# A recomputed written-out order for a fused attention and FFN kernel: other first loads, other eviction engines, other last semaphore

## Chip, core and metric

The kernel runs on one core of a Trainium2 chip. The metric is the device time of one execution in microseconds (us), lower is better. A profiled execution also has a span: the time from its first to its last recorded instruction.

## The reference, cut to what matters

For 8 batches of 8 heads, 576 queries attend to 16 beacon keys and, causally, to 576 keys of width 64. The result is laid out as 4608 rows of 512 and goes through a product of two linear layers and two more linear layers:

```python
k_all = np.concatenate([beacon_k, k], axis=2); v_all = ...      # (8, 8, 592, 64)
scores = scale * np.matmul(q, k_all.transpose(0, 1, 3, 2))      # causal mask after the 16 beacons
a = softmax(scores);  attn = np.matmul(a, v_all)
x = attn.transpose(0, 2, 1, 3).reshape(4608, 512)
h = ((x @ w1) * (x @ w2)) @ w3                                  # 1024 wide
out = h @ w_out                                                 # (4608, 512)
```

## The kernel before

The kernel multiplies `w3` by `w_out` first (Wt = w3·w_out), so that the FFN is `((x@w1)*(x@w2)) @ Wt`. All matmuls are in fp16 with fp32 sums. No loop runs over the work: a string `ORDER` of some two thousand small steps is read from left to right, and each step issues its instructions on a fixed engine. Every engine and every DMA queue takes its own instructions in the order in which the string names them; semaphores join the engines. So the order of the string is the whole schedule. The letters at the end of a step name an engine (`A` ScalarE, `D` VectorE, `P` GpSimd, `S` SyncE), the last number of a matmul step is the PSUM bank (0 to 7; a pair of banks for scores).

The steps, with their lines in the profile:

- Loads. `lq b c`, `lk b c`, `lv b c` load piece c of q, k or v of batch b (L332, L340), `lkb` and `lvb` the beacons (L369, L377, L385). For batch 0, q and k are loaded in another shape (L357), and the very first piece of each is loaded by the queues of SyncE and ScalarE, in fp32. `l1 c` and `l2 c` load a block of 256 columns of `w1` and `w2` (L390), `l3 r` a block of `w3` (L399), `lo a` a block of `w_out` (L402). All but the two first loads are on GpSimd's queue. It has eight semaphores, which its DMAs take in turn, so that a ninth waits for the first.
- Batch 0 and the weights. `cast` puts a loaded piece into fp16 order, `tq`/`tk` transpose it on TensorE (L422 for batch 0, L428 for others), `eq`/`ek` evict it (L296). `tn`/`en` do the same for beacons (L458). `t3 r`, `e3 r` transpose a block of `w3` (L484), `f r a` multiplies a part of it by `w_out` block a (L493), `ew r` evicts a row block of Wt.
- Attention. `s b g` computes group g of 13 score groups of a batch into a pair of banks with 64-row operands (L508), `exp` evicts it through ScalarE into a ring of 8 (L518), `m` masks the diagonal on VectorE (L528), `v b t h` multiplies by v and a ones column (L539), `n` normalises on VectorE (L550, L551). For later batches q and k are transposed by DMA on SyncE's queue (`Dq` L471, `Dk` L477), and so is the attention's output (`TX` L574; on TensorE for batches 0 to 2: `x` L565, `ex`).
- FFN. Rows are taken in nine blocks of 512. `a mc kf` and `b mc kf` are the two first products (L580, four matmuls each); `ea` evicts the one, scaled, to SBUF on ScalarE (L300) or VectorE (L302); `eb` multiplies it by the other on VectorE (L595). `o mc mt` multiplies by Wt (L601, eight matmuls), `eo` evicts (L300 or L302), `st` stores 128 rows (L615) by GpSimd's queue or SyncE's. The last `o` of the program is done in two halves of 256 columns.
- `spin n bank` issues n matmuls of zeros whose result nobody reads (L621).

At the end SyncE waits for the semaphores of all DMA queues and engines in nine instructions of two semaphores each, and then for the barrier (L693). The DMAs of the hardware queues (SyncE's and ScalarE's) take eight semaphores in turn as well; the waits name these eight in a fixed order from the second instruction to the ninth.

Of the kernel before, what the change touches and what calls it, by code (L numbers as in the profile page):

```python
# [62 lines left out]
consts 0; lq 0 0 S; lk 0 0 A; l3 2; consts 1; spin 8 7; l3 4; l3 3; lo 0; lkb 0 P; cast 0 0 q A;  # L63
lo 1; l3 0; consts 2; spin 1 7; tq 0 0 6; cast 0 0 k A; l3 1; eq 0 0 D 6; spin 3 7; tk 0 0 7;
ek 0 0 A 7; spin 2 6; t3 2 6; lq 0 1 P; e3 2 D 6; spin 2 7; t3 4 7; lkb 1; e3 4 D 7; spin 2 6;
t3 3 5; lo 2; e3 3 D 5; spin 2 7; f 4 0 6; lk 0 1 P; tn 0 7; f 2 0 5; lk 1 0 P; en 0 A 7; s 0 0 0;
s 0 1 2; lo 3; exp 0 0 0; f 2 1 5; f 4 1 6; f 3 0 7; exp 0 1 2; m 0 0 0; lv 0 4; s 0 2 0; f 3 1 7;
exp 0 2 0; m 0 0 1; t3 0 4; lk 0 2 P; t3 1 3; e3 0 D 4; cast 0 1 q A; lk 0 3 P; e3 1 D 3; f 0 0 2;
lq 0 2 P; tq 0 1 4; f 0 1 2; eq 0 1 A 4; l3 6; f 4 2 6; f 2 2 5; cast 0 1 k A; lvb 0; f 1 0 4;
l3 5; tk 1 0 3; f 1 1 4; ek 1 0 A 3; f 1 2 4; tk 0 1 3; lq 0 3 P; f 2 3 5; ek 0 1 A 3; lq 1 1 P;  # L70
f 3 2 7; ew 2 D 5; f 3 3 7; cast 0 2 k A; lkb 2; f 1 3 4; ew 3 D 7; f 4 3 6; lv 0 1; cast 0 3 k A;
tk 0 2 5; ew 1 D 4; f 0 2 2; lv 0 0; ek 0 2 A 5; cast 0 2 q D; tk 0 3 7; ew 4 D 6; tq 0 2 4;
ek 0 3 A 7; f 0 3 2; lk 1 4 P; eq 0 2 D 4; t3 6 6; ew 0 A 2; lv 0 3; s 0 3 0; s 0 4 4; s 0 5 2;
e3 6 D 6; exp 0 3 0; lvb 1; f 6 0 7; t3 5 6; cast 0 3 q D; lv 0 2; exp 0 5 2; m 0 1 0; f 6 1 7;
e3 5 D 6; f 6 2 7; l1 3; exp 0 4 4; s 0 6 0; s 0 7 2; m 0 1 1; l3 7; tq 0 3 6; exp 0 7 2; f 6 3 7;
lq 1 0 P; eq 0 3 D 6; f 5 0 5; l2 1; f 5 1 5; ew 6 D 7; exp 0 6 0; tk 1 4 6; f 5 2 5; l1 1;
ek 1 4 D 6; f 5 3 5; m 0 2 0; tq 1 1 6; l1 0; ew 5 A 5; eq 1 1 D 6; v 0 1 0 7; lq 1 3 P; v 0 0 1 5;
n 0 1 0 7; v 0 0 0 6; n 0 0 1 5; l2 0; s 0 8 2; s 0 9 0; s 0 10 4; n 0 0 0 6; lq 1 4 P; exp 0 8 2;
v 0 2 0 7; lk 1 3 P; t3 7 6; n 0 2 0 7; exp 0 10 4; v 0 1 1 3; lk 1 1 P; e3 7 D 6; tq 1 0 7;
exp 0 9 0; s 0 11 4; n 0 1 1 3; f 7 0 6; lq 1 2 P; f 7 1 6; m 0 2 1; exp 0 11 4; s 0 12 2;  # L80
eq 1 0 D 7; f 7 2 6; m 0 3 0; exp 0 12 2; v 0 2 1 7; l1 2; m 0 3 1; f 7 3 6; n 0 2 1 7; v 0 3 1 5;
ew 7 A 6; lk 1 2 P; v 0 3 0 4; n 0 3 1 5; tq 1 3 6; l2 3; n 0 3 0 4; x 0 1 7; eq 1 3 A 6; x 0 2 5;
x 0 3 3; ex 0 1 D 7; ex 0 2 A 5; x 0 4 6; x 0 0 4; lv 1 4; ex 0 3 D 3; ex 0 4 A 6; ex 0 0 D 4;
tq 1 4 7; l2 2; eq 1 4 A 7; a 0 3 5; lv 1 0; b 0 0 6; ea 0 3 A 5; lv 1 2; b 0 3 7; lv 1 3; a 0 1 5;
eb 0 3 7; tk 1 1 4; lq 2 0 P; ea 0 1 A 5; tk 1 3 7; ek 1 1 D 4; tq 1 2 3; b 0 1 2; ek 1 3 A 7;
lv 1 1; eq 1 2 D 3; tk 1 2 7; eb 0 1 2; a 0 0 5; ek 1 2 A 7; lk 2 0 P; a 0 2 7; ea 0 0 A 5;
lk 2 2 P; eb 0 0 6; s 1 0 0; s 1 1 2; s 1 2 4; ea 0 2 A 7; lq 2 2 P; exp 1 1 2; b 0 2 6; lq 2 1 P;
a 0 4 7; exp 1 2 4; m 1 0 1; lq 2 4 P; eb 0 2 6; b 0 4 3; exp 1 0 0; lk 2 1 P; ea 0 4 D 7; a 0 6 6;
eb 0 4 3; lk 2 3 P; s 1 3 4; s 1 4 0; s 1 5 2; m 1 0 0; ea 0 6 A 6; lq 2 3 P; exp 1 3 4; tq 2 0 7;
v 1 0 0 6; eq 2 0 D 7; lv 2 0; n 1 0 0 6; tk 2 0 7; exp 1 5 2; a 0 5 5; lk 2 4 P; ek 2 0 D 7;  # L90
m 1 1 0; exp 1 4 0; lk 3 2 P; tk 2 2 6; b 0 5 7; m 1 1 1; ek 2 2 D 6; lk 3 0 P; ea 0 5 A 5;
s 1 6 2; s 1 7 0; s 1 8 4; eb 0 5 7; exp 1 6 2; lv 2 1; Dq 2 4; v 1 1 0 6; tq 2 2 7; n 1 1 0 6;
lq 3 4 P; exp 1 8 4; tq 2 1 3; v 1 0 1 2; lv 2 3; eq 2 2 D 7; tk 2 1 6; eq 2 1 D 3; exp 1 7 0;
tk 2 3 7; lk 3 3 P; b 0 7 5; ek 2 1 D 6; ek 2 3 D 7; lkb 3; v 1 1 1 6; n 1 0 1 2; tq 2 3 7;
a 0 7 4; lv 2 4; n 1 1 1 6; eq 2 3 A 7; m 1 2 1; tk 2 4 7; lv 2 2; b 0 6 6; ea 0 7 A 4; ek 2 4 D 7;
m 1 2 0; lq 3 3 P; s 1 9 0; s 1 10 2; eb 0 7 5; exp 1 9 0; v 1 2 0 7; lvb 2; eb 0 6 6; o 0 1 5;
lk 3 1 P; n 1 2 0 7; exp 1 10 2; lq 4 1 P; m 1 3 0; v 1 2 1 7; eo 0 1 A 5; lq 3 1 P; s 1 11 0;
s 1 12 2; s 2 0 4; n 1 2 1 7; exp 1 11 0; st 0 1 P; Dk 3 2; v 1 3 0 6; lq 4 3 P; o 0 0 7;
n 1 3 0 6; exp 2 0 4; Dk 3 0; m 1 3 1; exp 1 12 2; m 2 0 0; s 2 1 0; s 2 2 4; s 2 3 2; eo 0 0 D 7;
Dq 3 3; exp 2 1 0; st 0 0 P; x 1 0 6; v 2 0 0 7; ex 1 0 D 6; exp 2 2 4; Dq 3 4; s 2 4 0; n 2 0 0 7;  # L100
v 1 3 1 6; m 2 0 1; o 0 2 7; exp 2 4 0; lvb 3; n 1 3 1 6; Dk 3 1; lq 3 2 P; exp 2 3 2; lv 3 0;
Dq 3 1; x 1 3 6; eo 0 2 D 7; x 1 2 5; ex 1 3 A 6; o 0 3 4; lq 3 0 P; ex 1 2 D 5; Dk 3 3; m 2 1 0;
st 0 2 P; lk 3 4 P; v 2 1 0 7; eo 0 3 A 4; x 1 1 6; n 2 1 0 7; lkb 4; x 1 4 5; v 2 0 1 3;
ex 1 1 A 6; lk 4 0 P; ex 1 4 D 5; s 2 5 0; s 2 6 4; n 2 0 1 3; exp 2 5 0; a 1 4 6; lk 4 1 P;
a 1 3 7; lv 3 1; exp 2 6 4; Dq 3 2; m 2 1 1; ea 1 4 D 6; lv 3 3; s 2 7 2; s 2 8 0; s 2 9 4;
ea 1 3 A 7; m 2 2 0; exp 2 7 2; b 1 4 6; v 2 2 0 7; lq 4 2 P; exp 2 9 4; eb 1 4 6; v 2 1 1 3;
Dq 3 0; n 2 2 0 7; a 1 0 2; exp 2 8 0; lv 3 2; n 2 1 1 3; b 1 0 6; ea 1 0 A 2; m 2 2 1; lv 3 4;
s 2 10 4; s 2 11 0; s 2 12 2; eb 1 0 6; Dk 3 4; lq 4 0 P; exp 2 10 4; b 1 1 7; m 2 3 0; lk 4 3 P;
exp 2 11 0; Dq 4 3; v 2 3 0 6; v 2 2 1 5; n 2 3 0 6; exp 2 12 2; a 1 1 4; Dk 4 0; n 2 2 1 5;
lq 5 1 P; x 2 0 6; ea 1 1 A 4; m 2 3 1; x 2 4 3; a 1 2 5; Dq 4 1; ex 2 4 D 3; ex 2 0 A 6; eb 1 1 7;  # L110
v 2 3 1 4; lk 4 2 P; b 1 3 6; Dk 4 1; n 2 3 1 4; b 1 2 7; eb 1 3 6; lkb 5; x 2 1 4; ea 1 2 A 5;
x 2 3 6; ex 2 1 D 4; ex 2 3 A 6; x 2 2 3; a 1 5 5; eb 1 2 7; lk 4 4 P; ex 2 2 A 3; a 1 6 6;
ea 1 5 D 5; Dq 4 2; s 3 0 0; s 3 1 2; s 3 2 4; ea 1 6 A 6; lq 4 4 P; exp 3 1 2; a 2 0 7; lv 4 3;
a 2 3 6; exp 3 2 4; m 3 0 1; ea 2 0 D 7; b 1 5 3; exp 3 0 0; lk 5 1 P; b 1 6 7; eb 1 5 3; Dq 4 0;
m 3 0 0; ea 2 3 A 6; s 3 3 4; s 3 4 0; s 3 5 2; eb 1 6 7; exp 3 3 4; lv 4 4; v 3 0 0 6; Dk 4 3;
a 1 7 7; n 3 0 0 6; exp 3 4 0; m 3 1 0; b 1 7 5; lvb 4; ea 1 7 D 7; exp 3 5 2; v 3 0 1 6; eb 1 7 5;
s 3 6 0; s 3 7 2; s 3 8 4; n 3 0 1 6; lv 4 1; exp 3 6 0; v 3 1 0 7; m 3 1 1; Dk 4 2; o 1 1 6;
lv 4 0; exp 3 8 4; m 3 2 0; n 3 1 0 7; lv 4 2; Dk 4 4; exp 3 7 2; m 3 2 1; v 3 2 0 7; lq 5 0 P;
eo 1 1 D 6; s 3 9 0; s 3 10 4; s 3 11 2; Dq 4 4; n 3 2 0 7; exp 3 9 0; v 3 1 1 6; st 1 1 P;
o 1 0 7; exp 3 10 4; m 3 3 0; n 3 1 1 6; exp 3 11 2; st 0 3 P; v 3 2 1 6; eo 1 0 D 7; v 3 3 0 5;  # L120
m 3 3 1; b 2 0 4; st 1 0 P; n 3 3 0 5; a 2 1 7; eb 2 0 4; TX 3 0; b 2 3 5; n 3 2 1 6; ea 2 1 A 7;
TX 3 4; b 2 1 7; eb 2 3 5; eb 2 1 7; s 3 12 0; s 4 0 2; s 4 1 4; exp 3 12 0; Dq 5 1; a 2 4 6;
exp 4 0 2; v 3 3 1 7; Dk 5 1; ea 2 4 D 6; s 4 2 0; s 4 3 2; lv 5 3; exp 4 1 4; m 4 0 0; a 2 6 6;
n 3 3 1 7; Dq 5 0; lq 6 3 P; exp 4 3 2; m 4 0 1; v 4 0 0 5; a 2 7 7; lk 5 2 P; ea 2 6 D 6; TX 3 3;
exp 4 2 0; m 4 1 0; o 1 2 4; lk 5 4 P; ea 2 7 D 7; lq 5 4 P; TX 3 2; n 4 0 0 5; lq 5 2 P;
v 4 1 0 7; eo 1 2 A 4; TX 3 1; lq 5 3 P; b 2 4 6; n 4 1 0 7; lk 5 0 P; a 2 2 5; eb 2 4 6; lvb 5;
b 2 2 7; ea 2 2 A 5; lk 5 3 P; b 2 6 6; eb 2 2 7; s 4 4 2; s 4 5 0; s 4 6 4; eb 2 6 6; exp 4 4 2;
lq 6 1 P; b 2 7 7; Dk 5 2; exp 4 6 4; lk 6 2 P; v 4 0 1 6; eb 2 7 7; o 1 3 3; Dk 5 4; lv 5 1;
exp 4 5 0; m 4 2 0; n 4 0 1 6; m 4 1 1; Dq 5 4; v 4 2 0 7; eo 1 3 A 3; st 1 2 P; s 4 7 4; s 4 8 0;
s 4 9 2; n 4 2 0 7; exp 4 7 4; Dq 5 2; b 2 5 6; st 1 3 P; exp 4 9 2; v 4 1 1 7; Dq 5 3; a 2 5 5;  # L130
n 4 1 1 7; exp 4 8 0; a 3 3 4; m 4 3 0; ea 2 5 A 5; Dk 5 0; m 4 2 1; b 3 2 7; eb 2 5 6; ea 3 3 A 4;
s 4 10 2; s 4 11 0; s 4 12 4; exp 4 10 2; Dk 5 3; b 3 3 6; exp 4 12 4; b 3 1 3; eb 3 3 6; Dq 6 3;
exp 4 11 0; a 3 0 2; Dq 6 1; v 4 2 1 6; m 4 3 1; ea 3 0 A 2; v 4 3 0 5; n 4 2 1 6; v 4 3 1 4;
Dk 6 2; a 3 5 2; n 4 3 0 5; lv 6 1; n 4 3 1 4; b 3 5 6; TX 4 0; ea 3 5 A 2; lv 5 4; lv 6 0;
# [56 lines left out]
def kernel(  # L191
# [13 lines left out]
    nc = tc.nc  # L205
    B, H, S, D = q.shape
    Nb = beacon_k.shape[2]
    P = 128
# [80 lines left out]
    def bank(n):  # L289
        return shape(n, "one")  # L290
# [407 lines left out]
```

## Time and profile before

| what | us |
|---|---|
| median of 5 runs | 292.9 (292.36 to 295.09) |
| time of the profiled execution | 293.42 |
| its span | 291.7 |
| TensorE busy | 284.6 |
| ScalarE busy / VectorE busy / GpSimd busy | 163.5 / 154.4 / 133.5 |
| first matmul of zeros / first score exponential | 1.26 / 14.02 |
| first FFN matmul (L580) | 43.23 |
| last eviction starts | 288.25 |

The time of the profiled execution is 1.7 us above its span, and 0.5 us above the median. A busy TensorE is not TensorE at its peak, since matmuls are pipelined and their ends are modelled; the distance from start to start is what a matmul costs in a dense stream.

### The profile page before, as it was taken

Reading aid. Unit: us, or ns where it says so; the run is one execution under the profiler, and the core shown is the slowest. Engines: PE = TensorE matmul, PEld = TensorE weight load, DVE = VectorE, ACT = ScalarE, POOL = GpSimd, SP = SyncE. Lnnn points to the kernel's source line nnn. Section 1 sums busy time; section 2 is a strip of 40 time slices with the busy share of each in tenths; the row PEclk is TensorE's granted clock in tenths of the full one; section 3 lists DMA queues with packets and bytes.
Section 4 is the critical chain, followed back from the end, with each engine's and each line's share of the span. In section 5 each row is a group of like instructions: output and inputs, shape, how many; then the busy total and the mean of one; then the engine's idle time right before and its main releaser. Section 6 shows DMA issues by size and latency. Waiting matters only on the chain.

```text
span 291.7 us, 7029 instructions
## 1 busy us (share of the span) xinstructions
PE 284.6 (98%) x2904; PEld 155.4 (53%) x2904; DVE 154.4 (53%) x344; ACT 163.5 (56%) x214; POOL 133.5 (46%) x186
## 2 busy tenths in 40 slices
PE   7999989999999999999999999999999999999995
PEld 2555755566656565565445545555455545444443
DVE  3338774786667577655456634634546653144500
ACT  3178664868685884477265626845475553232232
POOL 8569878997876460960966601940011001000000
PEclk9999999999999999999999999999999999999999
DMA  7999999999999999999999993999324014200033
GB/s 167 198 196 160 170 175 176 155 131 151 199 179 144 138 140 197 132 148 201 142 167 171 165 173 88 119 153 221 47 91 111 0 29 124 74 2 0 0 145 144
DMA packets 154319, 38.84 MB, mean 133 GB/s; under 512 B 144048, under 2 KB 149936, under 8 KB 154288
## 3 DMA queue, kind: packets, MB, share of 16 engines
q0 software_dynamic: 114720, 26.19, 104.1%
q1 hardware_dynamic: 39360, 11.92, 26.8%
q8 instruction: 22, 0.36, 0.5%
q10 hardware_dynamic: 208, 0.29, 0.3%
q14 instruction: 9, 0.07, 0.1%
HBM read 39.32 MB, written 9.44 MB: 167 GB/s over the span
## 4 chain that ended last, share of the span: by engine, by line
PE 84%; DMA 8%; POOL 5%; ACT 1%; issue 1%; DVE 0%; POOLq 0%
PE one L580 43%; PE one L601 21%; PE one L539 9%; PE pair L508 8%; DMA q<-in_q_dram 3%; DMA k<-in_k_dram 3%; DMA wo<-in_moe_w_out_dram 2%; PE one L428 1%; POOL va L340 1%; PE one L565 1%; POOL w L390 1%; POOL xT L399 1%; ACT ring L518 1%; POOL q L332 1%; POOL st L357 0%
## 5 line engine op out<-in xcount | busy, mean ns | idle before, releaser
L580 PE MATMUL one<-xT,w 128*128 128x512 f16 x576 | 133.0, 379 | 0.4 <-DVE xT L296 0.4
L518 ACT ACTIVATE ring<-pair 128x1024 f16<-128x1024 f32 x104 | 99.1, 1026 | 14.7 <-PE pair L508 14.4
L580 PEld LDWEIGHTS <-w 128*128 128x128 f16 x576 | 53.2, 98 | 60.1 <-issue 2.5
L595 DVE TENSOR_TENSOR gT<-one,asb 128x512 f16<-128x512 f32 x72 | 49.4, 690 | 55.1 <-PE one L580 41.1
L601 PE MATMUL one<-Wt,gT 128*128 128x512 f16 (+1 forms) x296 | 66.3, 373 | 0.0
L300 ACT ACTIVATE asb<-one 128x512 f32<-128x512 f32 x55 | 32.9, 598 | 58.9 <-PE one L580 37.3
L615 POOL DMA_DIRECT2D out_dram<-st x26 | 14.7, 566 | 68.2 <-DVE st L302 25.6
L601 PEld LDWEIGHTS <-gT 128*128 128x128 f16 x296 | 27.8, 98 | 30.3 <-issue 0.5
L340 POOL DMA_DIRECT2D va<-in_v_dram x40 | 34.1, 856 | 20.7 <-PE one L539 14.3
L539 PEld LDWEIGHTS <-ring 128*128 128x128 f16 x960 | 34.8, 98 | 9.8 <-issue 1.7
L539 PE MATMUL one<-va,ring 128*128 128x65 f16 x960 | 37.7, 193 | 0.1
L300 ACT ACTIVATE st<-one 128x512 f32<-128x512 f32 (+1 forms) x26 | 15.1, 581 | 34.4 <-PE one L601 34.4
L551 DVE TENSOR_TENSOR x<-one,rd 128x384 f16<-128x384 f32 (+1 forms) x64 | 31.4, 491 | 2.2
L340 POOL DMA_DIRECT2D k<-in_k_dram x35 | 29.9, 859 | 5.1 <-DMA k<-in_k_dram 1.5
L332 POOL DMA_DIRECT2D q<-in_q_dram x35 | 30.1, 864 | 2.9 <-DMA va<-in_v_dram 1.3
L508 PE MATMUL pair<-qT,kT 64*128 64x80 f16 (+4 forms) x736 | 30.1, 225 | 0.1
L508 PEld LDWEIGHTS <-kT 64*128 64x128 f16 x736 | 19.9, 95 | 13.9 <-issue 10.2
L528 DVE TENSOR_TENSOR ring<-ring,MD 128x768 f16<-128x768 f16 x32 | 17.7, 553 | 10.2 <-ACT ring L518 10.2
L550 DVE RECIPROCAL rd<-one 128x6 f32<-128x6 f32 (+1 forms) x64 | 11.8, 185 | 20.4 <-PE one L539 20.2
L528 DVE TENSOR_TENSOR ring<-ring,MX 128x384 f16<-128x384 f16 x32 | 11.3, 353 | 10.5 <-ACT ring L518 10.4
L493 PE MATMUL one<-wo,gT 128*128 128x512 f16 x56 | 14.9, 380 | 0.4 <-DVE gT L296 0.3
L302 DVE TENSOR_SCALAR asb<-one 128x512 f32<-128x512 f32 x17 | 11.7, 688 | 3.5 <-PE one L580 3.5
(60 smaller groups left out, 130.7 us busy)
## 6 DMA issues: line engine op xcount, KB each, us to landing
out_dram<-st POOLq DMA_DIRECT2D x26, 256.0 KB, 6.4
q<-in_q_dram POOLq DMA_DIRECT2D x28, 128.0 KB, 6.9
va<-in_v_dram POOLq DMA_DIRECT2D x24, 128.0 KB, 7.0
k<-in_k_dram POOLq DMA_DIRECT2D x21, 128.0 KB, 7.2
out_dram<-st SPq DMA_DIRECT2D x9, 256.0 KB, 2.0
xT<-in_moe_w_dram POOLq DMA_DIRECT2D x8, 256.0 KB, 6.2
w<-in_moe_w_dram POOLq DMA_DIRECT2D x8, 256.0 KB, 7.2
wo<-in_moe_w_out_dram POOLq DMA_DIRECT2D x4, 256.0 KB, 7.5
```

What stands on the lines that cost most here:

```text
L300: nc.scalar.activation(dst, src, AF.Copy, scale=by)
L332: nc.gpsimd.dma_start(dst[:rows, c], src[b, :, ds(c * P, rows), :].rearrange("h s d -> s h d"))
L340: nc.gpsimd.dma_start(dst[ds(p0, rows), c], src[b, :, ds(s0, rows), :].rearrange("h s d -> s h d"))
L493: nc.tensor.matmul(bank(n), wT(r)[:, a, rt % 2, :], wo16[:, rt, :], start=(rt == 0), stop=(rt == NFT - 1),)
L508: nc.tensor.matmul(shape(n, "pair")[:, hh, ds(col, w)], kT[ds(hh * 64, 64), t, ts(jt, P)], qT[ds(hh * 64, 64), t, ds(q0, w)],)
L518: nc.scalar.activation(held(b, g)[:, :, 0:GW], shape(n, "pair"), AF.Exp, scale=scale)
L528: nc.vector.tensor_tensor(blk, blk, msk, ALU.mult)
L539: nc.tensor.matmul(pv[:, 2 * at + hh, 0 : D + 1], held(b, g)[:, hh, ds(col, P)], va[:, jt, 2 * t + hh, 0 : D + 1], start=(jt == 0), stop=( ...
L551: nc.vector.tensor_tensor(x16s[b % NB2][:, ds(2 * h, ni), ts(t, P)].rearrange("p i (h d) -> p i h d", h=2), pv[:, 0 : 2 * ni, 0:D].rearran ...
L580: nc.tensor.matmul(bank(n), w12[:, kt, ds(i * DF + kf * P, P)], xT[:, kt, ds(mc * 512, 512)], start=(kt == 0), stop=(kt == NKT - 1),)
L595: nc.vector.tensor_tensor(gTs[mc % 2][:, kf, :], bank(n), asb[slot["asb", (mc, kf)]], ALU.mult)
L601: nc.tensor.matmul(bank(n)[:, 0:w], gTs[mc % 2][:, kf, ts(mt, P)], Wt[:, kf, ds(c0, w)], start=(kf == 0), stop=(kf == NFT - 1),)
```

## The change

The string `ORDER` is replaced by another one with the same work in it. The first load of k now goes to SyncE's queue and that of q to ScalarE's, the other way round from before. The order of the loads on GpSimd's queue, of the matmul groups, of the evictions and stores is new nearly everywhere, and so are many bank numbers. Counted over the string: matmuls of zeros 20 → 18 (and `spin` can now write into bank 0); `tk` transposes on TensorE 14 → 12, `Dk` by DMA 25 → 27; `ea` on ScalarE 55 → 36 and on VectorE 17 → 36; `eo` on ScalarE 26 → 21 and on VectorE 11 → 16; `cast` on VectorE 2 → 5; `e3` on ScalarE 0 → 3; `ew` on ScalarE 3 → 7; stores by GpSimd's queue 26 → 29 and by SyncE's 11 → 8. Runs of adjacent `s` groups, as TensorE sees them: 39 → 41. The eight semaphores of the hardware queues are taken in turn by the two first loads, the DMA transposes and SyncE's stores: 2 + 76 + 11 = 89 before, 2 + 78 + 8 = 88 now. So the last store took the first semaphore, which the second of the nine final waits names, and now takes the eighth, which the ninth names.

```diff
 ORDER = """
-consts 0; lq 0 0 S; lk 0 0 A; l3 2; consts 1; spin 8 7; l3 4; l3 3; lo 0; lkb 0 P; cast 0 0 q A;
-lo 1; l3 0; consts 2; spin 1 7; tq 0 0 6; cast 0 0 k A; l3 1; eq 0 0 D 6; spin 3 7; tk 0 0 7;
-ek 0 0 A 7; spin 2 6; t3 2 6; lq 0 1 P; e3 2 D 6; spin 2 7; t3 4 7; lkb 1; e3 4 D 7; spin 2 6;
-t3 3 5; lo 2; e3 3 D 5; spin 2 7; f 4 0 6; lk 0 1 P; tn 0 7; f 2 0 5; lk 1 0 P; en 0 A 7; s 0 0 0;
...
+consts 0; lk 0 0 S; lq 0 0 A; l3 3; consts 1; spin 8 7; lkb 1; lkb 0 P; l3 4; lk 0 1 P; lq 0 1 P;
+cast 0 0 k A; lo 0; consts 2; cast 0 0 q D; spin 2 7; tk 0 0 6; lo 1; tq 0 0 7; ek 0 0 A 6;
+eq 0 0 D 7; spin 1 0; t3 3 5; lvb 0; tn 0 6; lo 2; e3 3 A 5; l3 6; spin 3 7; t3 4 4; en 0 A 6;
+l3 0; s 0 0 0; s 0 1 2; e3 4 A 4; cast 0 1 k D; lk 0 3 P; tk 0 1 6; cast 0 1 q D; l3 2; exp 0 0 0;
...
+ex 0 3 D 6; ex 0 2 A 3; lv 1 2; s 1 0 0; s 1 1 4; s 1 2 2; ex 0 1 D 7; exp 1 0 0; a 0 4 6; l1 3;
+exp 1 1 4; m 1 0 0; l2 2; a 0 0 7; ea 0 4 D 6; l2 3; exp 1 2 2; tq 2 0 5; m 1 0 1; a 0 5 6;
...
+b 0 4 4; n 1 1 0 5; b 0 2 3; eb 0 4 4; lq 2 3 P; b 0 5 5; ea 0 2 A 6; ea 0 3 D 7; lk 2 3 P;
...
-o 7 0 7 0 256; eo 8 1 A 6; st 8 1 S; eo 7 0 A 7 0 256; st 7 0 S 0 256; o 7 0 5 256 256;
-eo 7 0 A 5 256 256; st 7 0 S 256 256
+eo 8 1 A 6; st 8 1 S; eo 8 0 A 7 0 256; st 8 0 S 0 256; o 8 0 5 256 256; eo 8 0 A 5 256 256;
+st 8 0 S 256 256
 """
...
     def spin(reps, n):
         for _ in range(reps):
-            nc.tensor.matmul(bank(n), zeros[:, 0:P], zeros)
+            nc.tensor.matmul(bank(n) if n else tiles[0][:, 0, :], zeros[:, 0:P], zeros)
```

## The prediction

> **What bounds the kernel now.** I read the page first, then the chain of waits in order of time, the groups of instructions, and last SyncE's waits.
>
> ```profile
> span 291.7 us, 7029 instructions
> PE 284.6 (98%) x2904; PEld 155.4 (53%) x2904; DVE 154.4 (53%) x344; ACT 163.5 (56%) x214; POOL 133.5 (46%) x186
> ...
> DMA  7999999999999999999999993999324014200033
> ...
> q0 software_dynamic: 114720, 26.19, 104.1%
> ```
>
> TensorE is busy nearly throughout, the eviction engines little over half. The DMA row is at 9 for the first 24 slices: GpSimd's load queue (q0) is full.
>
> ```profile
> 3.43 7.21 DMA wo<-in_moe_w_out_dram
> ...
> 11.58 8.09 DMA k<-in_k_dram
> ...
> 32.15 8.89 DMA q<-in_q_dram
> 41.08 0.40 PE one L428 x4
> ...
> 95.22 0.77 PE pair L508 x22
> 95.99 3.56 PE one L580 x16
> ...
> 110.47 3.46 PE one L580 x16
> ...
> 274.38 13.85 PE one L601 x72
> 288.25 0.38 ACT st L300
> ```
>
> The chain has two parts. Up to 41 us it runs over load landings: start plus duration says when a load is there, 10.64, 19.67 and 41.04 us. Counted along the string, 1024, 2480 and 6192 KB of GpSimd's stream have then landed: 161 and then 174 KB per us. This is my clock for loads. After 43 us it is TensorE alone to 288.2. One more thing is seen in it: the same 16 matmuls take 3.56 behind a run of score groups and 3.46 elsewhere. Leaving a run costs 0.10, and the third group of a run is as much longer than the others in the records: about 0.19 for each run.
>
> **TensorE's sum.** Start-to-start distances in a dense stretch: `a` and `b` 0.863 each (144), `o` 1.726 (35, and two halves of 0.873), `v` 0.367 and 0.548 (32 of each), `s` 0.22 to 0.24 (104), `f` 0.43 (32), `t3` 0.447 (8), small transposes 0.14 to 0.26, `spin` 0.216 (20). The sum is 270.1. To it come the start at 1.26; 39 score runs at 0.19, 7.4; and 4.9 for matmuls before 10.1 us, where the trace's clock record grants half speed (nine matmuls of zeros take 0.43 each). That is 283.6. The last matmul slot really ends at 288.05, so TensorE stands still for 4.4 in all. About 3.1 of it lies before 47 us (0.9 before the first transposes at 5.95, 0.5 for an eviction at 17, 0.7 and 0.5 around the landing at 41.04), 1.3 after.
>
> After: 18 matmuls of zeros and two `tk` of 0.22 fewer, 269.2; 41 runs, 7.8; cold part 4.6; start 1.26. That is 282.9, **0.7 less**. What then decides is how long TensorE stands still in the new order.
>
> **Loads.** I put the new load order on the landing record of the old (same cumulated KB, same time) and compare with the place of the first use in TensorE's unhindered sum. Up to 18 us every load is early by 0.3 to 2. Then it turns: `tk 1 2` at 29.9 needs KB 4672, there at 31.9; `tk 1 4` at 37.9 needs KB 6160, at 40.6; `b 0 0` at 46.8 comes 1.9 before its block; `b 0 4` at 49.8 needs the third `w2` block, KB 8240, which lands at 52.6 (the chain's own rate gives 41.04 + 2048/174 = 52.8). From there on the loads gain: `tk 2 2` 2.4, `tk 2 4` 2.4. These waits don't add up, the latest rules: TensorE stands still **2.8** up to `b 0 4`. What else is slow before it has this cover: the chain of six exponentials (1.03 each, from about 11.9 behind an `e3` on ScalarE) that makes banks free about 1 late at 18 us; no `e3` on ScalarE is in the trace, so I take its plain copies, 0.59 for 512 and 0.64 for 576 columns, which give about 1.0 for 1024, and at the least VectorE's 0.69. The cast of the first q on VectorE lies between VectorE's 0.35 (fp16 source) and ScalarE's 0.83 (fp32): either is over before q's transposes can start behind k's at 6.4. If the cover went, the exponentials would cost 1.0. The new `spin 2 0` writes bank 0 and so waits for the exponential of `s 0 3` (about 17.0, due 16.4), and `t3 0` and all of TensorE's queue behind it: 0.6 under the same cover.
>
> **Evictions.** The change moves 19 `ea` and 5 `eo` to VectorE.
>
> ```profile
> L518 ACT ACTIVATE ring<-pair 128x1024 f16<-128x1024 f32 x104 | 99.1, 1026 | 14.7 <-PE pair L508 14.4
> L300 ACT ACTIVATE asb<-one 128x512 f32<-128x512 f32 x55 | 32.9, 598 | 58.9 <-PE one L580 37.3
> L302 DVE TENSOR_SCALAR asb<-one 128x512 f32<-128x512 f32 x17 | 11.7, 688 | 3.5 <-PE one L580 3.5
> ```
>
> ScalarE is relieved of 24 × 0.6 = 14, VectorE takes 24 × 0.69 = 16.6 and gives some `ew`: about 150 and 169 of 292. In no stretch of 10 us after 40 us does either get over 9.5. So sums cost nothing; what costs are places where a bank is used again too soon. I compared each distance with eviction plus 0.25: after 55 us the new order is short at `s 3 4` (0.5), `s 1 9` (0.4), three `ea` on VectorE (0.1 each) and two `v` (0.2): 1.4 by sum. The same list for the old order gives 0.8 and the trace 1.3, of which 0.7 is dust of under 0.1. I take 1.0 + 0.7 = **1.7**; bounds 0.7 and 3.
>
> DMA transposes: SyncE's queue issues one each 1.3 and they land after 2.4 to 9. The tightest new uses are `s 3 0` (about 1.6 to spare), `s 7 0` and `a 5 1` (about 1, both within the error). I take 0, up to 2. Three more stores on GpSimd's queue and three fewer on SyncE's: 0.57 of issue each, at places where that queue has nothing due within 10 us; 0.
>
> **The end.** The last `o`, its eviction and its store keep their form.
>
> ```profile
> SPq L693 <- DMA out_dram<-st: 1.3, 1, 1.3
> SPq L693 <- PEq L693: 0.7, 2, 0.5
> ```
>
> The 1.3 is the landing of the last store. It is waited for by the second of nine instructions (released at 290.36 in the records), and the seven behind it come at 0.061 each. In the new order these seven are passed while the store is under way: **0.43 less**, the surest term. 3.65 from the last matmul slot to the end becomes 3.2.
>
> **Sum.** 282.9 + 2.8 + 1.7 + 3.2 = 290.6 against a span of 291.7: 1.1 less. The profiled execution took 293.42 and the median of the runs is 292.9; I carry the difference to the median: **291.8**.
>
> **Two rules of the skill.** (1) In the trace VectorE's copy of a batch-0 piece ran at 24.16 to 24.74 beside two v loads issued on GpSimd in 0.86 each, just the mean of that row (856 ns). The Trainium skill, "SBUF — State Buffer", section "SBUF: two separate sides", says that GpSimd can't write its descriptors while a VectorE copy holds the port pair that they share. That speaks against this change, which puts three more `cast` on VectorE where the load stream rules. By the rule 3 × 0.58 = 1.7 of the stream could be lost, and the gain of 1.1 would turn into a loss of 0.6; by the row nothing. I take the row, since up to eight loads are under way, and keep 1.7 for the range. (2) The clock: the record grants full speed at 10.1. "TensorE: Matmul & The Clock Gate", Part 1, says that the clock follows activity in a free-running window of about 3.4 us. The new order stands still for 0.4 instead of 0.9 before the first transposes. A grant one window earlier would save 1.7 of the cold part, one later would cost as much. The trace can't tell; either way `b 0 4` waits for 52.6, so I take 0.
>
> **Rivals.**
>
> *The stream's stalls vanish* (chance 0.2). A part of the old landing record is one-off: the load of k at 11.58 took 8.09 and landed 1.9 after its forerunner, where its size is worth 0.7. If that comes from what lay beside it and does not recur, all later landings are 1.2 earlier: 2.8 becomes 1.6, and with it the time 290.6. Against it: the stream has the same loads and the same full queue.
>
> *The stream comes late* (0.25, slower). The new order leans on the stream at over a dozen places and has 368 KB more ahead of the last needed `w2` block than the old (8240 against 7872 KB). From `tk 1 4` to `b 0 4` any further delay is passed on one to one. One more step like the 1.2 above, and the 1.7 of the port rule, makes 2.9: 291.8 + 2.9 = 294.7. It is slower by over 0.5% once the block lands after 52.6 + 1.1 + 1.5 = 55.2. For it: the queue's share of 104%. Against it: the rate held within 161 to 174 over 30 us.
>
> *The change doesn't do what it says* at the end: if another semaphore were the last to come, 0.43 is lost, 292.2. The built order has the last store on the last hardware semaphore, so 0.05, within the main case.
>
> **Chances.** About 0.5% (1.5 us) is what a measurement of this kernel can tell from no change. Main case 0.55: 291.8, own range 290.4 to 293.3, of which 0.2 is faster by over 0.5%, 0.33 within, 0.02 slower. First rival 0.2, all faster. Second 0.25: 0.22 slower, 0.03 within. Sum: faster 0.40, same 0.36, slower 0.24. The range that leaves out 2 in 10 goes from 289.4 (first rival, late stalls at their bound of 0.7, 0.2 for the spread of a median) to 295.0 (the second, 0.3 for that spread).
>
> **Right or wrong.** Right: the last `w2` block lands at 52 to 53.5 and L580 idles before it; about 41 short excesses at score runs; no TensorE wait over 0.6 after 60; SyncE's last data wait directly ahead of the barrier. Wrong: TensorE idle over 4 before 55 us (the stream), or waits of over 1 us on `TX` or DMA-transposed q and k (SyncE's queue), or on VectorE's `asb` (evictions).

## The result, and the profile after

| | before | after |
|---|---|---|
| median, us | 293.36 (74 runs) | 292.2 (39 runs) |
| lowest to highest | 291.59 to 296.98 | 291.1 to 295.71 |
| ratio of after to before | | 0.9964, 95% interval 0.9951 to 0.9977 |
| profiled execution / its span | 293.42 / 291.7 | 291.4 / 289.7 |
| last matmul slot ends / from there to the end of the span | 288.05 / 3.65 | 286.46 / 3.22 |

The changed kernel is faster by 0.36%, about 1.05 us. The ratio is that of the fast runs, which leaves out the one run of the 39 in the slower state; the quotient of the two medians is 0.9960. Forecast were 1.1 us and 291.8. The median of before over 74 runs is 0.46 above that of the first five, which is where the absolute figure missed by 0.4.

The page of the kernel after, parts 1 to 3, the lines that answer to those shown of before:

```profile
span 289.7 us, 6996 instructions
PE 283.3 (98%) x2894; PEld 153.7 (53%) x2894; DVE 169.4 (58%) x366; ACT 148.5 (51%) x190; POOL 135.3 (47%) x189
...
DMA  8999999999999999999999981799950111043003
...
q0 software_dynamic: 114960, 26.98, 101.8%
```

TensorE is as full as before with 1.3 us less of busy time. ScalarE and VectorE have changed places (163.5 and 154.4 before). The load queue fills the same first 24 slices. (`ORDER` has 1189 steps before and 1187 after, fewer than the two thousand that were given above.)

The chain of waits of the kernel after, in order of time (start, us, what), two windows:

```profile
9.35 8.28 DMA st<-in_k_dram
17.66 0.37 DVE o16k L296
...
43.34 1.83 PE one L580 x8
...
50.65 0.86 PE one L580 x4
51.51 0.36 PE one L539 x12
51.87 3.52 PE one L580 x16
```

```profile
279.91 6.72 PE one L601 x39
286.64 0.02 issue
286.66 0.38 ACT st L300
```

The chain before ran over load landings up to the one at 41.04. Here the last one is a piece of k at 17.63, and from there the chain runs over TensorE and its evictions. That doesn't mean that loads have stopped mattering: the third `w2` block lands at 51.73 in the trace's DMA records, and `b 0 4`, the group at 51.77, starts 0.05 later. In the timeline of TensorE:

```profile
51.35 0.53 PE L539 MATMUL one<-va,ring 128*128 128x65 f16 x12
51.77 2.55 PE L580 MATMUL one<-xT,w 128*128 128x512 f16 x11
```

From the `v` to `b 0 4` it is 0.43, where 0.37 is the undisturbed distance. So the wait for the block is only 0.06 here: TensorE has stood still at earlier places (for 0.2 us at 30.97, for a piece of k, among others) and comes just as the block lands.

Groups of instructions of the kernel after:

```profile
L518 ACT ACTIVATE ring<-pair 128x1024 f16<-128x1024 f32 x104 | 99.1, 1026 | 29.5 <-PE pair L508 28.8
...
L300 ACT ACTIVATE asb<-one 128x512 f32<-128x512 f32 x36 | 21.4, 603 | 58.1 <-DVE gT L595 27.1
...
L302 DVE TENSOR_SCALAR asb<-one 128x512 f32<-128x512 f32 x36 | 24.7, 690 | 20.9 <-PE one L580 20.5
```

The durations are those of before (1026, 603 and 690 ns); 19 evictions have moved. ScalarE now sits idle for 28.8 us waiting for scores, before for 14.4: relief that nobody needed.

What TensorE itself waited for, and SyncE's waits at the end (`SPq` is SyncE's sequencer), both of the kernel after (engine, line, releaser: us in total, times, longest):

```profile
PE one L565 <- ACT ring L518: 0.4, 1, 0.4
...
PE one L484 <- DMA xT<-in_moe_w_dram: 0.3, 1, 0.3
```

```profile
SPq L693 <- DMA out_dram<-st: 0.8, 1, 0.8
SPq L693 <- PEq L693: 0.7, 2, 0.5
```

After the first 20 us, no wait of TensorE is over 0.6. The wait for the last store was 1.3 and is 0.8, because the other waits of that place are passed in the meantime.

### The profile page after: what moved, and what is told of

Read it like the earlier page. It is cut to its first block, busy times and chain, and to the rows that moved or that the text cites. A ratio compares the mean times of both kernels' runs of the same rounds, so it can differ in the third digit from the quotient of the medians.

```text
span 289.7 us, 6996 instructions
## 1 busy us (share of the span) xinstructions
PE 283.3 (98%) x2894; PEld 153.7 (53%) x2894; DVE 169.4 (58%) x366; ACT 148.5 (51%) x190; POOL 135.3 (47%) x189
## 4 chain that ended last, share of the span: by engine, by line
PE 91%; DMA 3%; POOL 3%; ACT 1%; DVE 1%; issue 0%; POOLq 0%; DVEq 0%; ACTq 0%
PE one L580 44%; PE one L601 22%; PE one L539 10%; PE pair L508 9%; PE one L493 3%; DMA st<-in_k_dram 3%; PE one L428 1%; PE one L565 1%; POOL xT L399 1%; ACT ring L518 1%; PE one L484 1%; POOL wo L402 1%; PE one L422 0%; POOL st L357 0%; DVE qT L296 0%
## 5 line engine op out<-in xcount | busy, mean ns | idle before, releaser
L580 PE MATMUL one<-xT,w 128*128 128x512 f16 x576 | 134.4, 379 | 0.0
L518 ACT ACTIVATE ring<-pair 128x1024 f16<-128x1024 f32 x104 | 99.1, 1026 | 29.5 <-PE pair L508 28.8
L615 POOL DMA_DIRECT2D out_dram<-st x29 | 16.6, 572 | 93.9 <-ACT st L300 50.9
L300 ACT ACTIVATE asb<-one 128x512 f32<-128x512 f32 x36 | 21.4, 603 | 58.1 <-DVE gT L595 27.1
L302 DVE TENSOR_SCALAR asb<-one 128x512 f32<-128x512 f32 x36 | 24.7, 690 | 20.9 <-PE one L580 20.5
L551 DVE TENSOR_TENSOR x<-one,rd 128x256 f16<-128x256 f32 (+1 forms) x64 | 31.4, 491 | 2.2
L300 ACT ACTIVATE st<-one 128x512 f32<-128x512 f32 (+1 forms) x21 | 12.2, 581 | 35.3 <-PE one L601 35.3
L550 DVE RECIPROCAL rd<-one 128x4 f32<-128x4 f32 (+1 forms) x64 | 11.8, 184 | 13.5 <-PE one L539 11.1
L302 DVE TENSOR_SCALAR st<-one 128x512 f32<-128x512 f32 x16 | 11.1, 691 | 14.3 <-PE one L601 14.3
```

What stands on the lines that cost most here:

```text
L300: nc.scalar.activation(dst, src, AF.Copy, scale=by)
L302: nc.vector.tensor_scalar(dst, src, by, None, ALU.mult)
L518: nc.scalar.activation(held(b, g)[:, :, 0:GW], shape(n, "pair"), AF.Exp, scale=scale)
L551: nc.vector.tensor_tensor(x16s[b % NB2][:, ds(2 * h, ni), ts(t, P)].rearrange("p i (h d) -> p i h d", h=2), pv[:, 0 : 2 * ni, 0:D].rearran ...
L580: nc.tensor.matmul(bank(n), w12[:, kt, ds(i * DF + kf * P, P)], xT[:, kt, ds(mc * 512, 512)], start=(kt == 0), stop=(kt == NKT - 1),)
```

## Experiments

Every ratio is to the kernel before, timed on the same chip; the changed kernel's own 0.9964 is the other reference, from runs of its own, so two ratios with overlapping intervals are not told apart. Line numbers in three kernels are one less, since their string is a line shorter.

**The last semaphore, done alone and undone.** One store near the end on the other queue turns the count of hardware DMAs from 89 to 88 in the old order, or from 88 to 89 in the new.

```diff
 # b_tail: kernel before
-eo 6 2 A 6; st 6 2 S;
+eo 6 2 A 6; st 6 2 P;
 # a_notail: kernel after
-TX 7 1; st 6 2 P; eb 7 6 6;
+TX 7 1; st 6 2 S; eb 7 6 6;
```

> The order before with one store (`st 6 2`) moved from SyncE's queue to GpSimd's, so that the hardware queues carry 88 DMAs and the last store takes the semaphore that is waited for last. Theory (a fixed end term): 0.43 us less than before (0.15%), SyncE's waits behind the landing shrink from eight to one. Rival (the end is set by the landing and the barrier alone): no change.

> The changed order with one store (`st 6 2`) moved to SyncE's queue: 89 DMAs on the hardware queues, so the last store's semaphore is again the second one waited for. Theory: 0.43 us more than the changed kernel, about 0.6 us under before. Rival (the gain lies wholly in the order): as the changed kernel, 1.05 under before.

Measured: 0.9984 (0.9965 to 1.0003) and 0.9982 (0.9958 to 1.0006). The one gives 0.16% to the old order, the other takes 0.18% from the new; expected were 0.15% both times. Each interval alone still reaches no change. The trace is sharper. From the landing of the last store to the end of the span: 1.36 us before, 1.36 in the undone kernel, 0.92 after, 0.92 in the one done alone. That is 0.44, forecast 0.43. SyncE's last waits in the undone kernel:

```profile
SPq L693 <- DMA out_dram<-st: 1.3, 1, 1.3
```

What is left of the change without its semaphore is about 0.5 us, again with no change inside its interval.

**The evictions put back.** In FFN blocks 5 to 8, 16 `ea` and 9 `eo` go back from VectorE to ScalarE.

```diff
-Dk 7 3; a 5 7 6; m 6 3 0; ea 5 3 D 2;
+Dk 7 3; a 5 7 6; m 6 3 0; ea 5 3 A 2;
 ...
-exp 7 2 2; a 6 0 6; m 7 1 0; eo 5 2 D 7;
+exp 7 2 2; a 6 0 6; m 7 1 0; eo 5 2 A 7;
```

> The changed order with the 16 `ea` and 9 `eo` that it gives to VectorE in row blocks 5 to 8 put back on ScalarE (52 and 30 on ScalarE, near the 55 and 26 of before). Theory (evictions lie beside TensorE's work in this stretch): within 0.3 us of the changed kernel. Rival (the choice of engines is where the gain comes from): the gain of 1.05 us goes, 293.4. Other rival (VectorE's 0.69 against 0.60 costs at every close reuse of a bank): 0.3 to 1 us faster than the changed kernel.

Measured: 0.9966 (0.9945 to 0.9986), nearly the changed kernel's own value. The rival that the gain lies in the choice of engines is excluded, since the interval stays below 1; an effect of 0.3 us either way is not, since the interval reaches 0.6 us to both sides. But this kernel's one profiled execution has a span of 292.0, 2.3 more than that of the changed kernel (it is the slowest of its 22 runs, and the changed kernel's is the fourth fastest of 39). TensorE's waits in it say why:

```profile
PE one L484 <- DMA xT<-in_moe_w_dram: 1.3, 1, 1.3
...
PE pair L508 <- DMA kT<-k: 1.1, 1, 1.1
PE one L580 <- DMA xT<-x: 0.5, 1, 0.5
```

The first is a load in the first 20 us. Neither of the last two is an eviction. Both are DMA transposes that landed late, at places which the edit doesn't touch in the order of the queue. They led to the last experiment below.

**More load.** A second copy of the third `w2` block (256 KB) is loaded ahead of `l1 0`.

```diff
-exp 0 9 2; m 0 2 1; l1 0; s 0 11 0;
+exp 0 9 2; m 0 2 1; l2 2; l1 0; s 0 11 0;
```

> The changed order with the third block of w2 loaded twice, the additional 256 KB ahead of the first block of w1 in GpSimd's stream. Theory (from `tk 1 4` to `b 0 4` TensorE follows the stream): all later loads land 1.4 us later and so does everything behind them: 1.2 to 1.5 us more than the changed kernel. Rival (other waits decide and the loads have slack): under 0.4 us more.

Measured: 1.0014 (0.9985 to 1.0043), 0.5% or 1.46 us over the changed kernel. In the timeline of TensorE (start, us, engine, line, operation; in brackets the idle time before it and what ended it) the wait stands at the place that was forecast:

```profile
52.12 0.53 PE L539 MATMUL one<-va,ring 128*128 128x65 f16 x12
53.00 1.47 PE L580 MATMUL one<-xT,w 128*128 128x512 f16 x6 [0.35 <-DMA w<-in_moe_w_dram]
```

The block lands at 52.96 instead of 51.73, and `b 0 4` starts right behind it. So more load ahead of this block passes on to the time. The size fits what 256 KB are worth at the 174 KB per us of the old order (1.47 us), but the interval is some 0.9 us to either side.

**The first two queues.** Swapped back in the new order, and swapped alone in the old.

```diff
 # a_swap: kernel after
-consts 0; lk 0 0 S; lq 0 0 A;
+consts 0; lk 0 0 A; lq 0 0 S;
 # b_swap: kernel before
-consts 0; lq 0 0 S; lk 0 0 A;
+consts 0; lq 0 0 A; lk 0 0 S;
```

> The changed kernel with the first two loads on each other's queue again, k on ScalarE's and q on SyncE's. Theory (what the first 10 us gain or lose is swallowed at the load waits up to `b 0 4`): ratio 0.9964 within 0.001. Rival (the queue of the first k sets the start, and the start passes to the end): 0.3 us or more slower, ratio 0.9975 or above.

> The kernel before with its first two loads on each other's queue (q on ScalarE's, k on SyncE's), its order as it was. Theory (the start is swallowed at the load waits): ratio 1.0000 within 0.0015. Rival (the first queues themselves are the gain of the change, or the loss where the order is made for the other landing): 0.3 us or more, ratio below 0.999 or above 1.001.

Measured: 0.9971 (0.9943 to 0.9999) and 1.0002 (0.9976 to 1.0029). Both are within the theory, but the first interval is too wide to exclude a loss of 0.3 us. Its `b 0 4` starts at 52.26, inside what kernels with the new order show without the swap (51.69 to 52.48). The old order shows no gain from the other landing by itself.

**Less load ahead of the block, and a wait of 0.57 taken away.** The second edit was aimed at the longest late wait of the changed kernel, 0.57 over TensorE's own cost, of which the timeline shows 0.41 as idle:

```profile
99.24 0.62 PE L565 MATMUL one<-ident,x 128*128 128x128 f16 x8
100.26 0.38 PE L565 MATMUL one<-ident,x 128*128 128x128 f16 x4 [0.41 <-ACT ring L518]
```

```diff
 # a_relief
-lq 2 0 P; v 0 3 0 7; ... l2 3; exp 1 2 2; tq 2 0 5; ... eq 2 0 D 5;
-tk 2 2 6; b 0 3 7; ek 2 2 A 6; ... s 1 8 4; eb 0 3 7; exp 1 6 0; tq 2 1 6;
+v 0 3 0 7; ... l2 3; lq 2 0 P; exp 1 2 2; ...
+b 0 3 7; tk 2 2 6; ek 2 2 A 6; ... s 1 8 4; tq 2 0 6; eq 2 0 D 6; eb 0 3 7; exp 1 6 0; tq 2 1 6;
 # a_fix
-x 2 3 6; x 2 1 7; ... ex 2 1 D 7; exp 3 5 4; x 2 2 3; v 3 0 1 7; ... n 3 0 1 7; ... ex 2 3 A 6;
+x 2 3 6; ex 2 3 D 6; x 2 1 7; ... ex 2 1 D 7; v 3 0 1 6; exp 3 5 4; x 2 2 3; ... n 3 0 1 6; ...
 # a_best: both
```

> The changed kernel with one more load of q (part 0 of block 2, 256 KB) moved from ahead of the third w2 block to behind the fourth, and the transposes that need it, and those of k of part 2, moved behind `b 0 3`. Theory (the load stream sets when `b 0 4` runs): the third block lands about 0.8 us sooner than 52.4, and what is gained is what that leaves until the next load that TensorE waits for, 0.1 to 0.4 us: ratio 0.9950 to 0.9960. Rival (the stream isn't the bound there, the order behind it is): ratio 0.9964 as for the changed kernel, `b 0 4` starting no sooner. Also possible: the moved load is now late for its own transposes, ratio 0.997 or more, and a wait is then seen at `tq 2 0`.

> The changed kernel with the wait of 0.57 us near 99.5 us taken away: `x 2 2` into banks 3 comes behind `v 3 0 1`, so that `exp 3 4` has read its banks by then, and `ex 2 3` goes to VectorE right behind its matmul. Theory (a wait in mid kernel, with no load behind it, passes to the end at full size): the wait of 0.57 is gone, 0.5 us less, ratio about 0.9947. Rival (it turns up later, at `tq`, `s 7 0` or another consumer of transposed blocks, which come at their own time): ratio 0.9964, with as much standing still later.

> Both edits together: the later load of q with its transposes, and the other order near 99.5 us. Theory: the two gains add, 0.6 to 0.9 us less than the changed kernel, ratio 0.9933 to 0.9943. Rival (the waits for transposed q and k near 130 and 210 us, 0.2 to 1.3 us in the runs so far, take it back, since TensorE comes there sooner): ratio 0.9950 to 0.9964.

Measured: 0.9994 (0.9965 to 1.0023), 0.9956 (0.9931 to 0.9980), 0.9997 (0.9973 to 1.0021). The first expectation has the load as 256 KB; it is 128. The load edit failed, and neither by a late block nor by late transposes. `b 0 4` starts at 51.99 with its block there since 51.24. The loss comes 8 us later, in the first kernel's timeline of TensorE:

```profile
58.49 0.40 PE L428 MATMUL one<-ident,q 128*128 128x128 f16 x4
59.47 0.38 PE L428 MATMUL one<-ident,q 128*128 128x128 f16 x4 [0.58 <-DVE qT L296]
60.06 1.67 PE L580 MATMUL one<-xT,w 128*128 128x512 f16 x7 [0.21 <-DVE gT L595]
```

I had put two transposes one behind the other into bank 6. The second waits for VectorE to read the first, and the eviction behind it is late too: 1.1 us over TensorE's own cost at the two. The other edit took 0.11 of its 0.57: now `v 3 0 1` waits for `ex 2 3` (0.29 idle). Its 0.9956 is 0.0008 below the changed kernel, which the interval doesn't tell from nothing.

**The transposes' queue.** In the profiles so far, TensorE lost 0 to 1.27 us at `s 7 0` and 0 to 0.74 at `a 3 0`. Two transposes that have time are moved behind those that `a 3 0` needs, and one behind the last k piece that `s 7 0` needs:

```diff
 # a_sp: kernel after
-... Dq 7 3; exp 6 3 4; ... Dk 7 0; ... Dk 7 1; ... Dk 7 3; ... Dk 7 2;
+... exp 6 3 4; ... Dk 7 0; ... Dk 7 1; ... Dk 7 3; ... Dk 7 2; Dq 7 3;
-... Dq 5 3; ... Dk 5 3; ... TX 3 2; ... TX 3 1; ... TX 3 3;
+... TX 3 2; ... TX 3 1; ... TX 3 3; Dq 5 3; Dk 5 3;
 # a_best2: also the edit of a_fix, and
-eo 1 1 A 7;
+eo 1 1 D 7;
 # a_best3: also lq 2 0 behind l2 3, and "tq 2 0 5; eq 2 0 D 5;" behind "b 0 3 7;"
```

> The changed kernel with three DMA transposes that have time moved behind others that TensorE waits for on SyncE's queue: `Dq 7 3` behind `Dk 7 2`, `Dq 5 3` and `Dk 5 3` behind `TX 3 3`. Theory (the waits of 0.2 to 1.2 us at `s 7 0` near 210 us and of 0 to 0.7 us at `a 3 0` near 131 us in all runs so far are transposes that land late because of those ahead of them, and pass to the end): both waits gone, 0.3 to 1.2 us less, ratio 0.9925 to 0.9955. Rival (the transposes that land there are held by the traffic, not by those ahead on the queue, so the order does nothing): `kT` lands near 211 us as before, ratio 0.9964. Rival two (the moved `Dq 7 3` is then late for `s 7 1`): a wait seen there, ratio 0.9964 or more.

> The same, with the other order near 99.5 us: `v 3 0 1` in bank 6 ahead of `x 2 2`, `ex 2 3` on VectorE, and `eo 1 1` on VectorE so that `exp 3 4` starts sooner. Theory: the wait there falls from 0.57 to about 0.1 us and this adds to what the transposes give: 0.4 to 0.5 us below that kernel, ratio 0.991 to 0.9945. Rival: VectorE, with two evictions more, is late for the next consumer and gives it back; ratio as with the transposes alone.

> The same, with the load of q (part 0 of block 2) behind the fourth w2 block and its transposes in bank 5 behind `b 0 3`, where no other transpose wants the bank. Theory (the step that failed with this load before was the bank shared with `tq 2 1`, 1.0 us, and the load stream sets `b 0 4`): `b 0 4` starts 0.4 to 0.8 us sooner than without it, 0 to 0.4 us less at the end. Rival: TensorE's order from 30 to 50 us is itself late by as much, so that `b 0 4` no longer waits for its load: no difference.

Measured: **0.9927 (0.9899 to 0.9956)**, 0.9941 (0.9919 to 0.9963), 0.9962 (0.9942 to 0.9982). The first is the fastest version found, 291.48 us (290.98 to 291.91), below both kernels; its interval and that of the changed kernel overlap by 0.0005. The same place in three timelines of TensorE, the changed kernel, the one with the evictions put back, and this one:

```profile
209.65 0.62 PE L508 MATMUL pair<-qT,kT 64*128 64x112 f16 x12
210.21 1.90 PE L601 MATMUL one<-Wt,gT 128*128 128x512 f16 x8
```

```profile
210.92 0.33 PE L508 MATMUL pair<-qT,kT 64*128 64x112 f16 x8
212.34 0.25 PE L508 MATMUL pair<-qT,kT 64*128 64x80 f16 x4 [1.09 <-DMA kT<-k]
```

```profile
209.67 0.40 PE L507 MATMUL pair<-qT,kT 64*128 64x112 f16 x12
210.01 1.90 PE L600 MATMUL one<-Wt,gT 128*128 128x512 f16 x8
```

Twelve matmuls of `s 7 0` in one piece of 0.40 are the undisturbed case; 0.62 hides a wait of 0.2; in the middle fence the last four stand off. SyncE's queue of this kernel shows the new order of issues:

```profile
189.26 1.26 SPq L573 DMA_TRANSPOSE xT<-x  x1
190.63 10.19 SPq L476 DMA_TRANSPOSE kT<-k  x4
200.91 1.25 SPq L470 DMA_TRANSPOSE qT<-q  x1
```

In the changed kernel the moved transpose stands ahead of the four of k:

```profile
190.80 1.31 SPq L471 DMA_TRANSPOSE qT<-q  x1
192.21 7.88 SPq L477 DMA_TRANSPOSE kT<-k  x4
```

The last k piece is issued no earlier than there (199.52, against 198.08), but it takes 7.7 us to land instead of 11.9. It lands at 207.2, in the two kernels built on it at 208.4 and 208.1, and in the kernels with the queue as the change left it between 210.0 and 212.4. TensorE comes for it between 209.6 and 211.6. So the rival, that the order on the queue does nothing, is out; why a transpose with one less ahead of it takes so much less time to land is not shown. The old order has all of k there by 206.4 in each of its three profiles.

The times of the runs say the same without a trace. In the three kernels with the moved transposes the middle half of the runs lies within 0.5 to 0.65 us (6, 10 and 12 runs). In the eight with the queue as the change left it, it spreads over 0.95 to 2.06. The old order, timed three times, has 1.0 to 1.4, though its transposes land in time, so it must have another source of spread. The size of the gain is less sure than its cause: 0.9927 against 0.9964 is 1.1 us, the quotients of the medians (0.9937 against 0.9960) give 0.7.

The other two add nothing. On VectorE the eviction of the `o` doesn't help: `v 3 0 1` still waits 0.29. With the load moved, `b 0 4` starts 0.5 earlier than in the kernel without that (51.43 against 51.96), and `s 1 8` gives it back at once, in TensorE's timeline:

```profile
58.56 0.39 PE L507 MATMUL pair<-qT,kT 64*128 64x128 f16 x6 [0.56 <-DVE asb L301]
```

It needs the bank that the moved transpose has left to VectorE, whose queue holds other evictions. The rival of this run holds: TensorE doesn't wait for the block at all here, which has been there since 50.68.

## Why the prediction was right, step by step

The forecast was right by its size and by its main steps, and one term of its sum is wrong. The profiles of kernels with the new order from `b 0 4` to the end can be added up. TensorE's sum from there, by the distances of the prediction, is 233.1 us. "Late" is what the last slot's end has beyond that, "s 7 0" and "a 3 0" are TensorE's waits for transposes:

| | `b 0 4` starts | late | of it s 7 0 + a 3 0 | last slot to end | span |
|---|---|---|---|---|---|
| predicted | 52.6 | 1.7 | 0 | 3.2 | 290.6 |
| after | 51.77 | 1.6 | 0.2 | 3.22 | 289.7 |
| last semaphore undone | 52.48 | 2.1 | 0.7 | 3.66 | 291.4 |
| evictions put back | 52.41 | 3.3 | 1.9 | 3.2 | 292.0 |
| one block more | 53.00 | 1.4 | 0 | 3.2 | 290.7 |
| first queues swapped | 52.26 | 2.8 | 1.5 | 3.23 | 291.4 |
| transposes moved | 51.80 | 1.4 | 0 | 3.22 | 289.5 |

- **The end, −0.43.** Right: 3.22 against 3.65, and done alone and undone it shows 0.44 in the records. In the two kernels with 0.9956 and 0.9941 VectorE comes late to the barrier, and the end is 0.22 longer again (1.14 from the last landing); why is open.
- **TensorE's sum, −0.7.** It can't be separated by a run. With about 0.5 us left when the semaphore is undone, the measured change fits the two terms with the standing still about equal in the old and the new order.
- **The load stream, `b 0 4` at 52.6.** Right as the place in part, and 0.4 too late on average: 51.77, 52.48, 52.41 and 52.26 without the extra block have a mean of 52.2. `b 0 4` itself waits for its block with the semaphore undone (0.40), the evictions put back (0.29) and one block more (0.52), hardly in the changed kernel (0.06), and not at all with the first queues swapped or the transposes moved, where the last waits before it are for a piece of k at 41.9 and of v at 32.6. (With the semaphore undone the profile names a step of VectorE as what ended this wait, but that step read another bank, and the block had landed 0.05 before.) So loads hold TensorE up before this place in every profile, but not always this load. That every load up to 18 us is early did not come true either: `t3 0` waits near 17 us for its block of `w3` in ten of the eleven profiles with the new order, from 0.15 up to 1.51 us, and the later waits swallow it. The first rival's premise, that the step of 1.2 in the old landing record is one-off, holds in part: in the two other profiles of the old order that load of k landed at 18.42 and 19.01 instead of 19.67, and the same 8240 KB at 51.9 and 52.5 instead of 52.6. It was worth 0.4 here, not 1.2.
- **The stream comes late.** It didn't. The rule of the Trainium skill ("SBUF — State Buffer", section "SBUF: two separate sides"), by which three more casts on VectorE could cost 1.7, is not seen here at that size: the block lands earlier than the old record put it, with those casts in place. In the changed kernel's timeline one load issue lies beside the first cast of q on VectorE:

```profile
5.22 0.56 DVE L296 CAST o16q<-st 96x768 f16<-96x768 f32 x1 [1.53 <-DMA st<-in_q_dram]
5.28 0.61 POOL L402 DMA_DIRECT2D wo<-in_moe_w_out_dram  x1
```

It took 0.06 over the median of its group, the most of the seven issues that overlap one of the five casts. Taking the row was right, though it was thinner evidence than it was read as: of the two v loads, only the one issued at 23.73 (0.83 us) overlaps the copy at 24.16. No run moved the casts alone.
- **The clock.** In the records full speed is granted at 6.74 in the changed kernel, and in kernels with the same first steps at 5.43 (semaphore undone), 3.9 (wait at 99.5 changed) and 7.2 (transposes moved). Their `b 0 4` starts at 51.77, 52.48, 51.69 and 51.80, with no relation to the grant. Zero was the right value, and this fits the reason given, that the waits for loads swallow it. The records agree with the window of the Trainium skill ("TensorE: Matmul & The Clock Gate", Part 1): the full clock lasts 279.9, 283.3 or 286.7 us, whole steps of 3.41 apart. It doesn't decide anything here.
- **Evictions.** Right: nothing that could be measured. Busy times 148.5 and 169.4 where 150 and 169 were worked out; the new `e3` on ScalarE took 1.01 (estimate 1.0), the first q cast on VectorE 0.56 (bounds 0.35 and 0.83).
- **Late standing still, 1.7, and transposes, 0 up to 2.** This is the step that failed, hidden in the one profile of the changed kernel (1.6 and 0.2). Late without the transposes is 1.3 to 1.4 in every measured row, so 1.7 was a little high. The transposes were taken at 0, as "about 1 to spare, both within the error" for `s 7 0` and `a 5 1`. The spare time isn't there: over the five orders of the table with the queue unmoved `s 7 0` and `a 3 0` cost 0 to 1.9, 0.9 in the mean (1.0 with the three other kernels that left the queue as it was). The mark that was set for wrong, a wait of over 1 us on DMA-transposed k, is met in three kernels (idle for 1.09, 1.07 and 1.03), though not in the changed kernel's own profile. The earlier loads offset it, so that the sum came out right partly by luck, by two misses of 0.4 and 0.5. `a 3 0` was not on the list at all; `a 5 1` never waited noticeably.

That the changed kernel's profile is 0.8 below its median fits this: it had the earliest `b 0 4` and the second smallest wait of the five. The five profiled executions lie on average only 0.1 below the medians of their kernels, so their mean wait is not that of odd runs. Moving the transposes took out the waits in all three kernels that did it, and the best of them is 1.1 us (0.0037) below the changed kernel, where the table's mean would give 0.9. So the change loses at the transposes about as much again as it gains in all (0.9 in the mean against 1.05). This is an estimate: the table has one profile of each kernel, and the medians alone give 0.7 for moving the transposes.

## What to carry to other kernels

When an order is recomputed, ask of every queue that engines wait for, not only of the bounding one, when its last needed piece lands; "one us to spare" on a queue that lands 10 us after issue is none, and moving an unneeded item behind the needed ones cost nothing here. A fixed cost at the end is the surest gain to forecast, since no work comes behind it whose waiting could take it back. A single profile can lie 2 us from another of equal median; split its span into the few places where it can differ before reading an edit into it.

## What the runs showed of the hardware

- The DMA transposes issued near 195 us, beside loads and stores on GpSimd's queue, land 8 to 13 us after issue and in order, at irregular steps, in the kernels with the queue as the change left it. With the evictions put back, `Dk 7 1` landed at 204.2 and the next, `Dk 7 3`, at 210.1. A v load issued just ahead of both on GpSimd's queue (195.1) landed only at 211.0. What held both for those 6 us stays open.
- One transpose (1.3 us of issue) moved out of the way let the last k piece land some 3 us earlier (207.2 to 208.4 against 210.0 to 212.4), though it was issued no earlier.
- The grant of the full clock came between 3.9 and 7.2 us in the executions with the new order whose records have it. In this kernel it decided nothing.
- In the kernel with only the semaphore changed, the store of 128 rows issued at 284.28 took 4.3 us to land where others take 2.0. Its span had 3.83 from the last slot to the end, although from the last landing to the end it had the short 0.92. I had not expected a store at the quiet end of the program to be this irregular.
